# Padding one constant and the packs so that the large tiles begin at multiples of 128 bytes

## The chip, the core and the metric

The kernel runs on one core of one Trainium2 chip. The metric is the device time of one execution in microseconds, lower is better. The core has five engines with queues of their own: TensorE (PE in the profile; PEld is its loading of weights), VectorE (DVE), ScalarE (ACT), GpSimd (POOL) and SyncE (SP), which issues nearly all DMAs here.

## What is computed

A linear attention with a decay for each channel, over 4 sequences of 768 steps with 8 heads of 48 channels, and then two feed-forward layers on its 3072 rows of 384 numbers:

```python
for t in range(S):
    state = alpha[:, :, t, :, None] * state + np.einsum('bhd,bhe->bhde', k[:, :, t], v[:, :, t])
    y[:, :, t] = np.einsum('bhd,bhde->bhe', q[:, :, t], state)

h = x @ w_in                                   # layer 1: 384 -> 2048
x = np.maximum(0.01 * h, h) @ w_out            # 2048 -> 384
h = x @ w_in2                                  # layer 2, the same sizes
out = np.where(h > 0.0, h, np.exp(np.minimum(h, 0.0)) - 1.0) @ w_out2
```

The weights come as 64-bit floats, all else as 32-bit floats.

## The kernel before

**Feed-forward layers.** The 3072 rows are six blocks of 512 columns; the 2048 hidden channels are 16 slices of 128. Every number that goes into a product is split into a high and a low part, so each product takes three matmuls: high by high, low by high, high by low. One step (layer, block, slice) is nine matmuls into a bank `hp` (`ffn1_h`, L446; `ffn2_h`, L571), the nonlinearity and its split into `gh` and `gl` on ScalarE and VectorE, and nine matmuls from these into three banks (`ffn1_y`, L532; `ffn2_y`, L620; L635 in the very last block, with 384 columns). That is 864 matmuls for each product of each layer, 3456 in all, of which all but the last block's 144 have 512 columns (3312). Weights, `x`, `gh` and `gl` have the type fp32r (`F32R`), the attention's tiles plain 32-bit floats.

**Weights.** A slice of raw weights (3072 bytes per partition for each of its two matrices) is loaded into a staging tile (`stage1`, L720 to L722, five DMAs), turned into 32-bit floats by ScalarE and VectorE (p1, p2, and, j1, j2: L392, L397, L405, L408, L412) and split into the high and the low tile `w0_m`, `w1_m` (L415, L418). In layer 1, after the first four, slices take turns in the two staging tiles `x2t2` and `x2t3`; the second next slice can be loaded when L412 has read the present one.

**Attention.** A unit is 128 steps of one sequence, all heads; there are 24. Its decays, keys and queries come as one pack with 1541 floats per partition (`load_unit`, L121 on), its values as `vt` (`load_v`). The units 0 to 7 (`u < EARLY`) feed the first two blocks. From unit 8 on the pack is loaded in four DMAs, since two of the four head pairs have the halves of their keys swapped: L135 loads decays and the first keys, the two L138 the swapped halves, L139 the queries. Per unit, VectorE runs two scans (L169, L196) and scales keys and queries (L182 to L202), TensorE makes scores (`sc`, L211 and L274) and outputs, and ScalarE and VectorE write the result into an `x` tile. When a block's four units are done, `gather` (L385) moves rows of the `x` tile from partition to partition by DMA, six at once, and the block's L446 matmuls can begin. For the first two blocks SP issues every other one of the six, and ScalarE the rest. L360 subtracts the high part of the first blocks' outputs in the bank: one matmul whose 512 columns are four runs of 128 in an `x` tile.

**Order.** Up to about 340 us the order is written out by hand: the string `STARTUP` (L472) lists the steps, and every engine does its own ones in that order. Around the change SP's order is: the five loads of a slice, the pack and v of a unit (`more`), the next slice, the gather of a block. Each DMA is given one of eight completion semaphores in turn, so SP also waits, before a DMA, until the DMA eight earlier has landed.

**Tiles in memory.** A pool's tiles lie one behind the other in each partition, and each starts at the next multiple of 32 bytes. First come the constants (`ident`, `keep`, `d0`, `d1`, ..., `carried`, L62 to L70), then the 32 weight tiles, the six `x2t`, two `x` tiles, three `t`, two `gh`, two `gl`, three packs (also used for `span`, `stg` and `osb`), three `vt`, and the small ones of the attention (`pe`, `E`, `F`, `A`, `kn`, `S`, `T`). `carried` has 16 floats more than are written by L257, because L301 reads 64 columns from a head's 48. In the built program, bytes past a multiple of 128: weights, `x2t`, `x`, `t`, `gh`, `gl` 64; the three packs 64, 96 and 0; `vt` 32; `E` 0; `F` 32; `A`, `S` and `T` 64.

Of the kernel before, what the change touches and what calls it, by code (L numbers as in the profile page):

```python
# [8 lines left out]
F32 = mybir.dt.float32  # L9
# [10 lines left out]
def attention_two_layers_kernel(  # L20
# [12 lines left out]
    nc = tc.nc  # L33
    NT, DM = out.shape
    DFF = w1.shape[0] * 128
    D = HEAD_DIM
    H = DM // D
    C = CHUNK
    NU = NT // C
    NC = SEQ // C  # L40
    NP = H // 2
    PD = 2 * D
    PR = 64 + D
    KD = DM // 128
    KF = DFF // 128
    EXT = NP * (C + 1) + 1

    const = ctx.enter_context(tc.tile_pool(name="const", bufs=1))
    wts = ctx.enter_context(tc.tile_pool(name="wts", bufs=1))
# [4 lines left out]
    pack_p = ctx.enter_context(tc.tile_pool(name="pack", bufs=3))  # L54
# [8 lines left out]
    keep = const.tile([128, 2, C], I32, name="keep")  # L63
    d0 = const.tile([PR, EXT], F32, name="d0")
    d1 = const.tile([PR, EXT], F32, name="d1")
    bias = const.tile([PR, 2], F32, name="bias")
    outside = const.tile([PR, NU], F32, name="outside")
    far_sum = const.tile([PR, 2], F32, name="far_sum")
    near = const.tile([1, 1], I32, name="near")
    carried = const.tile([PR, NP * D + 16], F32, name="carried")  # L70

    both = [[wts.tile([128, 2 * DM], F32R, name=f"w{i}_{m}") for i in range(2)] for m in range(KF)]
    minus = both[KF - 1][0][0:PR, 0:PR]
# [22 lines left out]
    def constants():  # L96
# [4 lines left out]
        nc.vector.memset(d0, 0.0)  # L101
        nc.vector.memset(d0[:, 0:EXT:C + 1], 1.0)
        nc.vector.memset(d1, 0.0)
# [15 lines left out]
    st = {}  # L119

    def load_unit(u, first=False):  # L121
        t = pack_p.tile([PR, EXT + 2 * NP * C], F32, tag="pack", name="pack")
        if first:
            m = EXT + NP * C
            nc.sync.dma_start(t[:, 0:EXT], seqs[u, :, 0:EXT])
            nc.sync.dma_start(t[:, EXT:m], seqs[u, :, EXT:m])
            nc.sync.dma_start(t[:, m:], seqs[u, :, m:])
        elif u == 1:
            nc.sync.dma_start(t[:, 0:EXT], seqs[u, :, 0:EXT])
            nc.sync.dma_start(t[:, EXT:], seqs[u, :, EXT:])  # L130
        elif u < EARLY:
            nc.sync.dma_start(t, seqs[u])
        else:
            m, e = EXT + 2 * C, EXT + NP * C
            nc.sync.dma_start(t[:, 0:m], seqs[u, :, 0:m])  # L135
            dst, src = [a.rearrange("r (g h c) -> r g h c", g=2, h=2) for a in (t[:, m:e], seqs[u, :, m:e])]
            for h in range(2):
                nc.sync.dma_start(dst[:, :, h], src[:, :, 1 - h])  # L138
            nc.sync.dma_start(t[:, e:], seqs[u, :, e:])  # L139
        packs[u] = t  # L140

    def load_spare(u):
# [19 lines left out]

    def prep_E(u):
        t = packs.pop(u)
        al, kq = t if isinstance(t, tuple) else (t[:, 0:EXT], t[:, EXT:])
        kS = kq[:, 0:NP * C].rearrange("p (g c) -> p g c", c=C)
        qh = kq[:, NP * C:].rearrange("p (g c) -> p g c", c=C)
        E = at_p.tile([PR, EXT], F32, tag="E", name="E")
        nc.vector.tensor_tensor_scan(E[:, ::-1], al[:, ::-1], d0[:, ::-1], 0.0, ALU.mult, ALU.add)  # L169
        st[u] = dict(kS=kS, qh=qh, alpha=al, E=E)  # L170
# [17 lines left out]
    def prep_k(u):  # L188
        prep_E(u)
        prep_pe(u)  # L190
        prep_kS(u)
# [512 lines left out]
    def next_load(u):  # L704
        if u < NU:
            load_unit(u)
            load_v(u)
        else:
            t = pack_p.tile([128, 2 * 768], I32, tag="pack", name="stg")
            slots2.extend([(t[:, 0:768], 99), (t[:, 768:1536], 99)])  # L710
            fill2()
# [203 lines left out]

    with ExitStack():
        load_unit(0, True)
        constants()
        load_unit(1)
        load_v(0)  # L920
        load_unit(2)
# [26 lines left out]
        def early_h(j, m, ahead=0):  # L948
# [3 lines left out]

        first = {
            "E": prep_E, "pe": prep_pe, "kS": prep_kS, "F": prep_F, "q": prep_q, "sc": lambda u: (attn_scT if u >= EARLY else attn_sc)(u), "pk": attn_pk, "X": attn_X,
            "kn": attn_kn, "pu": attn_pu, "po": attn_po, "T": attn_T, "S": attn_state, "carry": attn_carry,
            "mask0": lambda u: mask_half(u, 0), "mask1": lambda u: mask_half(u, 1),
# [28 lines left out]
        for s, e in enumerate(seq):  # L985
            ph, j, m = e
# [13 lines left out]
            if after >= 0:  # L1000
                quota = 4 * 33 * (after + 1) // PACE - flow.n if after < PACE else 0
                if after == 0:
                    t = x2t[NT // 512 - 1].rearrange("p c f -> p (c f)").bitcast(I32)
# [38 lines left out]
            if ph == 2 and m >= KF - 10 and m % 2 == 0:  # L1042
                u = 5 * j + (m - KF + 10) // 2
# [95 lines left out]
```

## Time and profile before

| | us |
|---|---|
| median of 3 runs | 917.37 (916.95 to 919.85) |
| the profiled execution | 920.86 |
| its span, first to last instruction | 919.1 |
| TensorE busy | 892.4 |
| VectorE, ScalarE busy | 531.4, 455.6 |
| mean granted clock of TensorE | 0.995 of full speed |

TensorE is the engine with the most work, and the one whose instructions make up most of the chain that ended last. The first 150 us hold the attention's first units, the loads of the first layer's weights and their conversion, all at once; behind them TensorE works nearly without a break. "Busy" of TensorE is from start to a modelled end, and matmuls overlap; the spacing of two matmuls is read from their starts. A granted clock of 1.0 is 2.4 GHz, 0.5 is 1.2 GHz.

### The profile page before, as it was taken

The numbers are of one execution on the slowest core, as the hardware profiler recorded it, in microseconds if no ns is written. First come the engines' busy times: TensorE is split into PE (matmuls) and PEld (weight loads), VectorE is DVE, ScalarE is ACT, GpSimd is POOL, SyncE is SP. The second block draws the span as 40 slices with busy tenths as digits, with TensorE's granted clock in tenths as the row PEclk, the third lists the DMA queues.
The fourth block names the chain that finished last, engine by engine and source line by source line (L and its number), as shares of the span: only waits on it lengthen the run. The fifth ranks groups of instructions, "written<-read, shape, count | busy, mean of one in ns | idle before, by whom it ended". The sixth has DMA issues, their size and how long they took to land.

```text
span 919.1 us, 13668 instructions
## 1 busy us (share of the span) xinstructions
PE 892.4 (97%) x5306; PEld 735.0 (80%) x5306; DVE 531.4 (58%) x894; ACT 455.6 (50%) x841; POOL 11.8 (1%) x36
## 2 busy tenths in 40 slices
PE   8898999999899999989999999999999999999997
PEld 6676787888778877878888888888888888888896
DVE  8896888845564656455378888533443443443432
ACT  3476565332223222322367788656556565566442
POOL 1010000000000000000000000000000000000000
PEclk9999999999999999999999999999999999999999
DMA  9865452241113131221334241211200200300201
GB/s 223 201 173 153 129 147 78 65 101 44 44 44 79 44 87 28 52 78 36 103 90 117 74 116 48 41 37 29 55 11 21 54 11 21 55 20 1 36 1 38
DMA packets 69386, 64.01 MB, mean 70 GB/s; under 512 B 43904, under 2 KB 50560, under 8 KB 69312
## 3 DMA queue, kind: packets, MB, share of 16 engines
q1 hardware_dynamic: 68448, 61.87, 26.9%
q10 hardware_dynamic: 864, 1.18, 0.4%
q8 instruction: 44, 0.72, 0.3%
q14 instruction: 30, 0.25, 0.1%
HBM read 54.37 MB, written 4.72 MB: 64 GB/s over the span
## 4 chain that ended last, share of the span: by engine, by line
PE 82%; DVE 7%; DMA 6%; ACT 2%; SPq 1%; issue 1%; POOL 0%; DVEq 0%; ACTq 0%; POOLq 0%
PE hp L571 21%; PE y L532 17%; PE hp L446 16%; PE o L620 11%; PE oa L620 7%; PE oa L635 3%; DMA x2t<-in_w_dram 2%; PE po L292 2%; DMA vt<-in_vals_dram 2%; DMA pack<-in_seqs_dram 2%; PE sc L274 1%; DVE A L239 1%; DVE gl L464 1%; PE o L635 1%; ACT gh L460 1%
## 5 line engine op out<-in xcount | busy, mean ns | idle before, releaser
L446 PE MATMUL hp<-x,w 128*128 128x512 f32 x864 | 216.8, 393 | 4.0 <-DMA x<-x 2.6
L571 PE MATMUL hp<-x,w 128*128 128x512 f32 x864 | 212.3, 390 | 0.0
L446 PEld LDWEIGHTS hp<-x,w 128*128 128x128 f32 x864 | 161.9, 189 | 41.3 <-DMA x<-x 3.6
L571 PEld LDWEIGHTS hp<-x,w 128*128 128x128 f32 x864 | 161.9, 188 | 33.3 <-DVE w L418 0.2
L532 PE MATMUL y<-gh,w 128*128 128x512 f32 x576 | 170.2, 395 | 0.0
L584 DVE SCALAR_TENSOR_TENSOR t<-t,hp 128x512 f32<-128x512 f32 x96 | 65.9, 686 | 143.6 <-ACT t L579 143.1
L460 ACT CAST gh<-t 128x512 fp32r<-128x512 f32 x96 | 59.7, 623 | 144.9 <-PE y L532 103.7
L464 DVE TENSOR_TENSOR gl<-t,gh 128x512 fp32r<-128x512 f32 x96 | 65.9, 689 | 103.5 <-ACT gh L460 97.1
L532 PEld LDWEIGHTS y<-gh,w 128*128 128x128 f32 x576 | 106.1, 188 | 22.6 <-ACT gh L460 0.5
L595 DVE TENSOR_TENSOR gl<-t,gh 128x512 fp32r<-128x512 f32 x96 | 66.5, 693 | 66.5 <-ACT gh L589 66.5
L532 PE MATMUL y<-gl,w 128*128 128x512 f32 x288 | 102.6, 392 | 0.4 <-DVE gl L464 0.4
L451 ACT COPY t<-hp 128x512 f32<-128x512 f32 x96 | 56.2, 586 | 89.8 <-PE hp L446 84.3
L578 ACT ACTIVATE t<-hp 128x512 f32<-128x512 f32 x96 | 57.3, 597 | 80.9 <-PE hp L571 80.7
L589 ACT CAST gh<-t 128x512 fp32r<-128x512 f32 x96 | 59.7, 622 | 70.2 <-PE o L620 22.8
L620 PE MATMUL o<-gh,w 128*128 128x512 f32 x288 | 88.7, 389 | 0.1
L456 DVE SCALAR_TENSOR_TENSOR t<-t 128x512 f32<-128x512 f32 x96 | 65.5, 685 | 35.0 <-ACT t L451 34.8
L532 PEld LDWEIGHTS y<-gl,w 128*128 128x128 f32 x288 | 53.6, 188 | 12.7 <-DVE gl L464 1.4
L620 PEld LDWEIGHTS o<-gh,w 128*128 128x128 f32 x288 | 54.0, 188 | 11.6 <-ACT x2t L553 0.5
L579 ACT ACTIVATE t<-t 128x512 f32<-128x512 f32 x96 | 60.7, 632 | 3.1
L620 PE MATMUL oa<-gh,w 128*128 128x512 f32 x192 | 59.1, 389 | 0.0
L620 PE MATMUL o<-gl,w 128*128 128x512 f32 x144 | 56.0, 389 | 0.0
L620 PEld LDWEIGHTS oa<-gh,w 128*128 128x128 f32 x192 | 36.0, 188 | 7.4
(134 smaller groups left out, 883.8 us busy)
## 6 DMA issues: line engine op xcount, KB each, us to landing
stg<-in_w_dram SPq DMA_DIRECT2D x28, 384.0 KB, 3.1
x2t<-in_w_dram SPq DMA_DIRECT2D x20, 384.0 KB, 4.3
span<-in_seqs_dram SPq DMA_DIRECT2D x24, 226.2 KB, 2.6
pack<-in_seqs_dram SPq DMA_DIRECT2D x16, 338.2 KB, 3.4
x2t<-in_w_dram SPq DMA_DIRECT2D x32, 144.0 KB, 2.8
pack<-in_seqs_dram SPq DMA_DIRECT2D x18, 224.0 KB, 3.0
out_dram<-osb SPq DMA_DIRECT2D x60, 64.0 KB, 2.0
pack<-in_seqs_dram SPq DMA_DIRECT2D x5, 674.2 KB, 9.8
```

The source lines that it names most:

```text
L446: nc.tensor.matmul(hp, lhsT=a[:, kk, :], rhs=x[:, kk, :n], start=(0 in halves and i == 0), stop=(1 in halves and i == len(terms) - 1))
L456: nc.vector.scalar_tensor_tensor(out=t, in0=t, scalar=0.01, in1=t, op0=ALU.mult, op1=ALU.max)
L460: nc.scalar.copy(gh, steps["t", j, m])
L464: nc.vector.tensor_sub(gl, steps.pop(("t", j, m)), steps["gh", j, m].bitcast(F32))
L532: nc.tensor.matmul(ytiles[j][c], lhsT=a[:, c * 128:(c + 1) * 128], rhs=x, start=(first and 0 in halves and c not in begun), stop=(last and ...
L571: nc.tensor.matmul(hp, lhsT=a[:, kk, :], rhs=x[:, kk, :], start=(i == 0), stop=(i == 3 * KD - 1))
L578: nc.scalar.activation(t, hp, ACTF.Relu, scale=-1.0)
L579: nc.scalar.activation(t, t, ACTF.Exp, scale=-1.0)
L584: nc.vector.scalar_tensor_tensor(out=t, in0=t, scalar=-1.0, in1=hp, op0=ALU.add, op1=ALU.max)
L589: nc.scalar.copy(gh, t)
L595: nc.vector.tensor_sub(gl, t, gh.bitcast(F32))
L620: nc.tensor.matmul(otiles[j][c], lhsT=a[:, c * 128:(c + 1) * 128], rhs=x, start=(m == 0 and i == 0), stop=(m == KF - 1 and i == 2),)
```

## The change

`carried` gets 16 floats more, so that the tiles behind the constants begin 64 bytes later; and a pack's row gets 27 floats that nothing uses (1568 instead of 1541). The DMAs that wrote the whole tile now name its first 1541 floats. Nothing is computed otherwise.

```diff
+    END = EXT + 2 * NP * C
-    carried = const.tile([PR, NP * D + 16], F32, name="carried")
+    carried = const.tile([PR, NP * D + 32], F32, name="carried")
...
     def load_unit(u, first=False):
-        t = pack_p.tile([PR, EXT + 2 * NP * C], F32, tag="pack", name="pack")
+        t = pack_p.tile([PR, END + 27], F32, tag="pack", name="pack")
...
-            nc.sync.dma_start(t[:, m:], seqs[u, :, m:])
+            nc.sync.dma_start(t[:, m:END], seqs[u, :, m:])
...
-            nc.sync.dma_start(t[:, EXT:], seqs[u, :, EXT:])
+            nc.sync.dma_start(t[:, EXT:END], seqs[u, :, EXT:])
         elif u < EARLY:
-            nc.sync.dma_start(t, seqs[u])
+            nc.sync.dma_start(t[:, 0:END], seqs[u])
...
-            nc.sync.dma_start(t[:, e:], seqs[u, :, e:])
+            nc.sync.dma_start(t[:, e:END], seqs[u, :, e:])
...
-        al, kq = t if isinstance(t, tuple) else (t[:, 0:EXT], t[:, EXT:])
+        al, kq = t if isinstance(t, tuple) else (t[:, 0:EXT], t[:, EXT:END])
```

In the built program weights, `x2t`, `x`, `t`, `gh`, `gl`, packs and `vt` then begin at multiples of 128 bytes. The tiles behind them move too: `E` goes from 0 to 96 past such a multiple, `F` from 32 to 0, `A`, `S` and `T` from 64 to 32.

The order of the instructions stays the same on every engine, and so does what they do, but for a memset of `carried` with 32 instead of 16 columns. Waits change, because the builder finds other overlaps between two DMAs into one pack. On SP, at the load of unit 8 (here `pack_834`), before the change; `DMAHW0` to `DMAHW7` are the eight completion semaphores, and each DMA's own is the first one named where it waits for the DMA eight earlier:

```order
L135 DMA pack_834<-in_seqs_dram 112x773 [waits DMAHW3_49,PE_49]
L138 DMA pack_834<-in_seqs_dram 112x2x64 [waits DMAHW4_49]
L138 DMA pack_834<-in_seqs_dram 112x2x64 [waits DMAHW5_49,DMAHW4_49]
L139 DMA pack_834<-in_seqs_dram 112x512 [waits DMAHW6_49]
L155 DMA vt_839<-in_vals_dram 128x2x144 [waits DMAHW7_49]
L157 DMA vt_839<-in_vals_dram 64x288 [waits DMAHW0_49]
L157 DMA vt_839<-in_vals_dram 64x288 [waits DMAHW1_49]
L720 DMA x2t3_138<-in_w1_dram 48x768 [waits DMAHW2_49,DVE_49]
```

And with the change (lines are one further on):

```order
L136 DMA pack_834<-in_seqs_dram 112x773 [waits DMAHW3_49,PE_49]
L139 DMA pack_834<-in_seqs_dram 112x2x64 [waits DMAHW4_49]
L139 DMA pack_834<-in_seqs_dram 112x2x64 [waits DMAHW5_49]
L140 DMA pack_834<-in_seqs_dram 112x512 [waits DMAHW6_49]
L156 DMA vt_839<-in_vals_dram 128x2x144 [waits DMAHW7_49]
L158 DMA vt_839<-in_vals_dram 64x288 [waits DMAHW0_49]
L158 DMA vt_839<-in_vals_dram 64x288 [waits DMAHW1_49]
L721 DMA x2t3_138<-in_w1_dram 48x768 [waits DMAHW2_49,DVE_49]
```

The second of the two half-swapped loads waited for `DMAHW4`, on which the first one lands; now it does not. It is so for each of the units 8 to 23. On TensorE, the scores of unit 9 (`pack_1029`), before:

```order
L274 MATMUL sc0_1301<-pack_1029 64x128
L274 MATMUL sc1_1302<-pack_1029 64x128
L274 MATMUL sc0_1301<-pack_1029 64x128 [waits DMAHW1_49,DMAHW0_49]
L274 MATMUL sc1_1302<-pack_1029 64x128
L274 MATMUL sc0_1301<-pack_1029 64x64
L274 MATMUL sc1_1302<-pack_1029 64x64
```

and with the change:

```order
L275 MATMUL sc0_1301<-pack_1029 64x128
L275 MATMUL sc1_1302<-pack_1029 64x128
L275 MATMUL sc0_1301<-pack_1029 64x128 [waits DMAHW1_49]
L275 MATMUL sc1_1302<-pack_1029 64x128
L275 MATMUL sc0_1301<-pack_1029 64x64 [waits DMAHW0_49]
L275 MATMUL sc1_1302<-pack_1029 64x64
```

The wait for one of the two loads stands two matmuls later, at the first that reads what it brings.

## Rows read from the trace of the kernel before

**Rows 1.** The page: busy time of each engine; shares of the chain that ended last.

```profile
PE 892.4 (97%) x5306; PEld 735.0 (80%) x5306; DVE 531.4 (58%) x894; ACT 455.6 (50%) x841; POOL 11.8 (1%) x36
...
PE 82%; DVE 7%; DMA 6%; ACT 2%; SPq 1%; issue 1%; POOL 0%; DVEq 0%; ACTq 0%; POOLq 0%
```

**Rows 2.** Stretches from:to, their length, busy us of each engine, clock, DMA.

```profile
core 0: us, PE busy (x) PEld busy (x) DVE busy (x) ACT busy (x) POOL busy (x), PEclk, DMA share, GB/s
...
70.60:77.40 6.80, 4.25 (x11) 2.82 (x11) 2.19 (x4) 2.72 (x4) 0.00 (x0) 0.75 0.71 170
77.40:97.00 19.60, 19.60 (x88) 16.17 (x88) 15.71 (x22) 12.25 (x20) 0.48 (x1) 1.00 0.59 163
97.00:125.00 28.00, 26.60 (x140) 20.29 (x139) 24.40 (x35) 19.94 (x32) 0.00 (x0) 1.00 0.36 106
125.00:146.00 21.00, 20.74 (x91) 16.65 (x90) 17.43 (x26) 12.35 (x19) 0.32 (x1) 1.00 0.50 140
```

**Rows 3.** The chain that ended last, 20 to 78 us: start, us, what.

```profile
21.17 9.46 DMA pack<-in_seqs_dram
...
30.65 10.09 DMA vt<-in_vals_dram
...
57.54 4.57 DMA pack<-in_seqs_dram
...
63.47 4.87 DMA vt<-in_vals_dram
...
68.83 4.44 DMA x<-x
...
73.32 4.08 PE hp L446 x9
```

**Rows 4.** Two stretches of TensorE alone: length, busy (matmuls), clock, DMA.

```profile
73.60:76.90 3.30, 3.30 (x8) 0.50 0.70 194
560.00:640.00 80.00, 80.00 (x353) 1.00 0.18 40
```

**Rows 5.** Waits of SP's queue: us in total, times, longest.

```profile
SPq L138 <- DMA pack<-in_seqs_dram: 48.2, 16, 4.7
```

**Rows 6.** SP's queue in time: start, us, what.

```profile
57.54 4.92 SPq L138 DMA_DIRECT2D pack<-in_seqs_dram  x2
...
64.78 0.52 SPq L720 DMA_DIRECT2D x2t<-in_w_dram  x1
...
67.69 0.42 SPq L722 DMA_DIRECT2D x2t<-in_w_dram  x1
```

**Rows 7.** ScalarE in time: start, us, what, [idle before, ended by].

```profile
65.55 0.59 ACT L364 CAST x<-po 112x512 fp32r<-112x512 f32 x1 [0.58 <-PE po L360]
...
66.55 0.91 ACT L397 ACTIVATE x2t<-x2t 128x768 int32<-128x768 uint16 x1
67.90 2.50 ACTq L385 DMA_DIRECT2D x<-x  x3
72.67 0.89 ACT L392 ACTIVATE x2t<-x2t 128x768 f32<-128x768 f32 x1 [5.21 <-DMA x<-x]
```

**Rows 8.** VectorE in time, around the same place.

```profile
61.26 0.96 DVE L412 CUSTOM_DVE_ANT_0 x2t<-x2t,x2t 128x1536 uint16<-128x1536 uint16 x1
...
74.07 0.69 DVE L456 SCALAR_TENSOR_TENSOR t<-t 128x512 f32<-128x512 f32 x1 [3.75 <-ACT t L451]
```

**Rows 9.** TensorE in time: one L360 and the matmul that follows.

```profile
55.65 0.40 PE L360 MATMUL po<-x,w 112*112 112x512 f32 x1
55.89 0.26 PE L219 MATMUL pk<-ident,pack 112*128 112x112 f32 x1
```

**Rows 10.** One line's instructions, L196, 200 to 345 us: ns min/median/max, first and last start.

```profile
L196 DVE TENSOR_TENSOR_SCAN F<-pack,d x7: 1222/1224/1227, 222.7 to 337.8; 112x516 f32<-112x516 f32 x7
```

**Rows 11.** The same view of L813, loads into the packs' slots, 595 to 830 us.

```profile
L813 SPq DMA_DIRECT2D span<-in_seqs_dram x19: 312/313/447, 599.6 to 823.2; - x19
...
DMA to landing us min/median/max: 2.4/2.6/2.8
```

**Rows 12.** The page's groups: matmuls of both layers, busy and mean ns, idle before.

```profile
L446 PE MATMUL hp<-x,w 128*128 128x512 f32 x864 | 216.8, 393 | 4.0 <-DMA x<-x 2.6
L571 PE MATMUL hp<-x,w 128*128 128x512 f32 x864 | 212.3, 390 | 0.0
```

## The prediction

> **What bounds the kernel now.** The first view is the page's busy times and the shares of its chain [rows 1]: TensorE works 892.4 of 919.1 us and holds 82% of the chain that ended last. So only two things can move the end: what each matmul takes, and the 26.7 us in which TensorE idles. The second view, the stretches [rows 2], says where it idles early on: in 70.60 to 77.40 TensorE is busy 4.25 of 6.80 us and its mean granted clock is 0.75; in 77.4 to 97 it is busy all of the time; it idles 1.40 us in 97 to 125, and 0.26 in 125 to 146. The third, the chain [rows 3], names who held it in the first of these: a pack load issued at 57.54, a v load at 63.47, the gather x<-x at 68.83 and then nine matmuls at 73.32 that take 4.08 us. Eight matmuls in 73.6 to 76.9 ran at a granted clock of 0.50, which is the 1.2 GHz level, after TensorE had idled 2.55 us [rows 2, 4]. The fourth view is one long steady stretch [rows 4]: 353 matmuls in 80.00 us, 226.6 ns each, where 512 columns at one a cycle and 2.4 GHz are 213.3 ns: 13.3 ns too many, and the place where a start of 64 bytes past a multiple of 128 could hide.
>
> **Part 1, the waits that go.** The padded pack row changes what the builder takes for overlapping. For each of the 16 units from 8 on, the second of the two half-swapped key loads (L138) no longer waits until the first has landed. SP held 48.2 us in that wait, 16 times [rows 5]. What it is worth depends on who waits behind it.
>
> The first one, at 57.54. SP is in the two L138 issues for 4.92 us, all but some 0.8 of it the wait; behind it stand the rest of the pack, v, weight slice 5 (L720 to L722) and SP's half of the gather [rows 6]. Without the wait SP comes to L720 at about 60.3. There it waits for DVE's L412 to free the staging tile, 61.26 + 0.96 = 62.2 [rows 8], so slice 5 starts at 62.25 instead of 64.78, and its last load (67.69 before) goes out near 64.1 [rows 6]. The gather's source is written by ACT's L364, done at 65.55 + 0.59 = 66.1; SP can issue its half from there instead of 68.83 [rows 3, 7]. ACT issues the other half and is free only at 66.55 + 0.91 = 67.5, against 67.90 [rows 7]. So ACT's half now comes last. How long it takes to land: 4.44 us before, behind slice 5's big load [rows 3]; 2.6, the median of a load in a quiet stretch [rows 11], at best. Slice 5 would be 3.5 us ahead, so I take 2.9, nearer the quiet row: landing near 70.4 (between 70.1 and 71.9). TensorE's work ahead of it is done at 73.32 - 2.55 = 70.8. Of the 2.55 us of idle time, between 1.3 and all goes; I take 2.4. With no idle stretch ahead of it the clock should stay at the higher level, which gives back 4.08 - 2.04 (nine times 226.6 ns) = 2.04 us, or nothing if it falls anyway. Together 4.4 (1.3 to 4.6).
>
> Who is late next? ACT waited 5.21 us for slice 5 before L392 at 72.67, and DVE 3.75 behind it [rows 7, 8]; both start about 3.4 us earlier now. TensorE gains 4.4, so it may have to wait up to 1.0 for them; two banks for hp give it 2.04 us of work in between. I take off 0.7: **3.7 us (1.0 to 4.6)**.
>
> The second and third waits, at 83 and 125, stand while TensorE is full (19.60 of 19.60, 20.74 of 21.00 [rows 2]): worth nothing by themselves. But weight slices arrive earlier behind them, which feeds ACT and DVE in 97 to 146, where TensorE idles 1.66 us in all. Between 0 and 1.7; I take 0.5. The other 13 stand after 146, where units are loaded well ahead: 0. The wait that moves two matmuls later on TensorE meets a DMA long landed: 0.
>
> **Part 2, the starts of the tiles, on TensorE.** Weights, x, gh and gl go from 64 bytes past a multiple of 128 to 0. Is that the 13.3 ns? If a read went in pieces of 128 bytes, 2048 bytes from 64 would take 17 pieces where 16 would do, and one piece is 32 columns, 13.3 ns: the number fits exactly. But one kind of matmul tests it: L360 reads its 512 columns as four runs of 512 bytes, each starting at 64, and would take 20 pieces, 267 ns. The next matmul starts 0.24 us after it (55.65 and 55.89 [rows 9]). So the 13.3 ns comes once per matmul and not once per start; I take 0 for the change, and keep the rest as a rival.
>
> The Trainium skill ("TensorE: Matmul & The Clock Gate", Back-to-back issue gap) gives N / 2.4 + 2.5 ns for a warm gap, 215.8 ns for 512 columns, and measured it on bf16. This trace has 226.6, so the measurement decides here; by that rule, if the starts were the whole difference, the change would be worth 36 us on 3312 matmuls and end near 877.
>
> **Part 3, the starts on the other engines and DMA.** Packs already lie at three different starts (64, 96 and 0 past 128; 192, 224 and 0 past 256), and units take them in turn. Seven scans over the three take 1222 to 1227 ns, and 19 loads into them land in 2.4 to 2.8 us [rows 10, 11]. So the starts cost VectorE nothing, and by its nearness I take nothing for ScalarE. For DMA the spread is 0.2 around 2.6, 8% either way: on the pack and v loads of 9.46 and 10.09 us that stand in the chain before 42 us [rows 3] that is up to 1.5 us better or worse; I take 0.
>
> The Trainium skill ("DMA: Bandwidth & Descriptors", How a descriptor splits into AXI transactions) lets a transaction start only at multiples of 256 bytes, so a 3072-byte row from 192 would be 13 of them instead of 12. By that rule the early loads would be some 8% shorter, which is the better end of the bound just given; the loads into three starts show no such order.
>
> Sum: 3.7 + 0.5 = 4.2 us off, between 1.0 - 1.5 = -0.5 and 4.6 + 1.7 + 1.5 = 7.8. The profiled execution took 920.86 (span 919.1) and would take 916.7; it lay 0.4% above the median of the runs, 917.37. Taken off the median: **913.2**.
>
> **Rivals.** *The head start is given back* (no change, 917.4, or 915 to 919): TensorE comes 4 us earlier to slices whose weights DVE and ACT have not split yet, and idles there instead. For it: DVE is busy 24.40 of 28.00 us in 97 to 125, ACT 19.94 [rows 2]. Against it: both sat idle 3.75 and 5.21 us for the same late loads. Unprofiled runs that never dropped the clock at 73.6 would also have only half of it to gain.
>
> *TensorE's 13.3 ns was the start after all* (869): 3312 x 13.3 ns = 44 us, and the 4.2. For it stands the fit of 32 columns; against it L360.
>
> *TensorE's reads collide* (slower, 923): all big tiles, packs and v now begin at the same place modulo 128, where packs and v lay at 96, 0 and 32 before. The matmuls of the first layer, among pack and v traffic, already last 393 ns where the second layer's last 390 [rows 12]. Another 3 ns on 3312 matmuls costs 9.9 us, against the 4.2. It decides for slower from (4.2 + 2.75) / 3312 = 2.1 ns per matmul. Against it: weights, x and g keep their distances from each other, as they all move by 64.
>
> *The change does not do what it says*: the built program has the starts at 0 as stated, so this is out.
>
> **How the numbers follow.** 0.3%, about what a measurement of this kernel can tell from no change, is 2.75 us. Forecast (4.2 off, 2.8 to 7.8): 0.55. Given back, or only half of it real: 0.27. The 13.3 ns gone: 0.08. Collisions or DMA made worse: 0.10. Faster 0.55 + 0.08 = 0.63, same 0.27, slower 0.10. The range leaves out the 869 and most of the slower case, and reaches from the sum's better end, 917.4 - 7.8 = 909.6, over no change to 919.4, where the given-back case (2 us worse at most) ends.
>
> **What would show it.** Right: in the changed kernel SP issues both L139 loads back to back near 57.5; TensorE starts the matmuls after the gather near 70.7 with no idle stretch, nine of them in 2.04 us, and no stretch at clock 0.50 near 74; ACT's L393 no longer idles 5 us before it; in steady stretches 226.6 ns per matmul stays, and the scans stay at 1225. Wrong: a pitch below 220 (the starts were it) or above 228 (collisions); or the same start at 70.7 but idle time that comes back between 77 and 146.

## The result, and the profile after

The changed kernel took 909.49 us (median of 4 runs, 908.50 to 911.75) against 918.23 us for the kernel before (4 runs, 916.95 to 919.85): a ratio of 0.9914, 95% interval 0.9887 to 0.9940, or 8.7 us off. In a second comparison it took 911.42 us (12 runs, 909.94 to 915.79) against 917.40 (23 runs, 914.50 to 920.83): 0.9942, 0.9923 to 0.9961, 6.0 us off. So it is faster, as both intervals leave out no change. The first interval, 5.5 to 10.4 us off, lies above the 4.2 us of the forecast; the second, 3.6 to 7.1, holds them.

The first comparison's profiled execution of the change took 911.75 us, its span is 910.0. The page of the changed kernel (its line numbers are one higher than before's), as [rows 1] of before:

```profile
PE 887.2 (97%) x5306; PEld 733.5 (81%) x5306; DVE 531.6 (58%) x894; ACT 455.8 (50%) x841; POOL 11.8 (1%) x36
...
PE 87%; DVE 5%; DMA 4%; SPq 1%; ACT 1%; issue 1%; POOL 0%; DVEq 0%; ACTq 0%; POOLq 0%
```

TensorE's busy time fell by 5.2 us, and its share of the chain rose from 82 to 87%. The stretches of the changed kernel, as [rows 2, 4] (from:to, length, busy us of each engine, clock, DMA):

```profile
57.50:70.60 13.10, 13.10 (x96) 10.57 (x97) 12.41 (x20) 8.88 (x16) 2.62 (x1) 1.00 0.72 195
70.60:77.40 6.80, 6.80 (x32) 5.63 (x31) 5.32 (x8) 5.25 (x8) 0.00 (x0) 1.00 0.60 158
77.40:97.00 19.60, 19.60 (x89) 16.21 (x88) 17.93 (x28) 14.41 (x22) 0.48 (x1) 1.00 0.58 148
97.00:125.00 28.00, 27.44 (x147) 22.01 (x146) 24.59 (x34) 18.09 (x28) 0.32 (x1) 1.00 0.61 165
125.00:146.00 21.00, 21.00 (x161) 17.48 (x160) 18.15 (x28) 11.83 (x18) 0.00 (x0) 1.00 0.19 60
560.00:640.00 80.00, 80.00 (x354) 66.06 (x353) 35.56 (x56) 50.46 (x91) 0.00 (x0) 1.00 0.15 34
```

The stretch 70.6 to 77.4 is full, at a granted clock of 1.00, with 32 matmuls begun where [rows 2] had 11 at 0.75. The steady stretch has not moved: 354 matmuls in 80.00 us, as the 353 of [rows 4]. So nothing happened to a matmul itself.

How the wait's end travels through the queues is seen on four engines. SP in time, changed kernel:

```profile
56.03 0.93 SPq L139 DMA_DIRECT2D pack<-in_seqs_dram  x2
57.00 0.45 SPq L140 DMA_DIRECT2D pack<-in_seqs_dram  x1
...
60.71 0.33 SPq L721 DMA_DIRECT2D x2t<-in_w_dram  x1
...
62.48 1.76 SPq L723 DMA_DIRECT2D x2t<-in_w_dram  x1
64.63 2.38 SPq L386 DMA_DIRECT2D x<-x  x3
```

VectorE in time:

```profile
59.72 0.96 DVE L413 CUSTOM_DVE_ANT_0 x2t<-x2t,x2t 128x1536 uint16<-128x1536 uint16 x1
...
69.18 0.69 DVE L457 SCALAR_TENSOR_TENSOR t<-t 128x512 f32<-128x512 f32 x1 [0.39 <-ACT t L452]
```

ScalarE in time:

```profile
64.02 0.59 ACT L365 CAST x<-po 112x512 fp32r<-112x512 f32 x1 [0.58 <-PE po L361]
...
64.64 0.61 ACTq L386 DMA_DIRECT2D x<-x  x1
65.02 0.91 ACT L398 ACTIVATE x2t<-x2t 128x768 int32<-128x768 uint16 x1
65.29 1.25 ACTq L386 DMA_DIRECT2D x<-x  x2
67.75 0.92 ACT L393 ACTIVATE x2t<-x2t 128x768 f32<-128x768 f32 x1 [1.82 <-DMA x2t<-in_w_dram]
```

The six DMAs of that gather (L386, 60 to 76 us), where before has 4.3/4.7/5.0:

```profile
DMA to landing us min/median/max: 3.0/3.4/3.9
```

TensorE in time, at the gather and where [rows 2] idled in 97 to 125:

```profile
68.28 0.94 PE L533 MATMUL y<-gl,w 128*128 128x512 f32 x3
69.06 4.27 PE L447 MATMUL hp<-x,w 128*128 128x512 f32 x18
...
92.89 1.52 PE L447 MATMUL hp<-x,w 128*128 128x512 f32 x6
```

The two swapped loads go out in 0.93 us, where [rows 6] has 4.92. Weight slice 5 starts at 60.71, right when L413 has freed the staging tile (59.72 + 0.96), and SP's half of the gather at 64.63, right when L365 has written its source (64.02 + 0.59): the two limits that the prediction had named as next. The matmuls after the gather follow the ones before without idle time, eighteen of them in one piece, where [rows 3] has the gather in the chain and nine in 4.08 us.

**A ruler for the rest.** The 5306 matmuls come in the same order in all the kernels here, so the start of the n-th one (counted from 0) can be compared between traces. Number 400 starts near 45 us, 614 is the last one ahead of the gather's matmuls and 622 the eighth of these, and 713 to 940 covers 97 to 146 us in before. Times between starts, in us:

| profile | start of 400 | 400 to 614 | 614 to 622 | 622 to 713 | 713 to 800 | 800 to 940 | 940 to last | 400 to last |
|---|---|---|---|---|---|---|---|---|
| before | 46.65 | 23.72 | 6.18 | 20.89 | 22.45 | 26.46 | 766.16 | 865.84 |
| before, again | 44.32 | 23.72 | 6.19 | 21.48 | 22.19 | 26.99 | 766.07 | 866.65 |
| the change | 45.14 | 23.69 | 1.85 | 20.63 | 20.63 | 25.79 | 766.02 | 858.60 |
| the change, again | 44.24 | 23.70 | 1.85 | 20.63 | 21.21 | 25.79 | 766.12 | 859.30 |
| waits only | 49.96 | 23.72 | 1.83 | 20.63 | 20.55 | 25.76 | 766.21 | 858.71 |
| waits only, again | 43.58 | 24.17 | 1.94 | 20.65 | 21.05 | 25.76 | 766.07 | 859.64 |
| starts at 96, no waits | 43.54 | 23.70 | 1.84 | 20.63 | 20.95 | 25.75 | 766.29 | 859.16 |
| first wait gone | 43.61 | 23.86 | 1.83 | 20.63 | 21.95 | 25.90 | 766.14 | 860.31 |
| first wait kept | 43.52 | 23.72 | 6.04 | 21.62 | 20.93 | 25.76 | 766.14 | 864.21 |
| starts only, all waits | 47.27 | 23.71 | 5.30 | 20.90 | 22.07 | 25.80 | 766.18 | 863.95 |

The last column parts the kernels cleanly: 866.2 on average for before, 858.6 to 859.6 for every kernel without the waits, whatever its starts. The difference of the means is 7.2 us: 4.3 at the gather, 0.6 up to matmul 713, 1.4 and 1.0 in the two columns after it, less 0.1 ahead of the gather, and nothing behind matmul 940. The column that scatters is the first: at matmul 400 the two profiles of before differ by 2.3 us, those of the change by 0.9, and those of the waits-only kernel by 6.4.

### The profile page after: what moved, and what is told of

Read it like the earlier page. It is cut to its first block, busy times and chain, and to the rows that moved or that the text cites. A ratio compares the mean times of both kernels' runs of the same rounds, so it can differ in the third digit from the quotient of the medians.

```text
span 910.0 us, 13650 instructions
## 1 busy us (share of the span) xinstructions
PE 887.2 (97%) x5306; PEld 733.5 (81%) x5306; DVE 531.6 (58%) x894; ACT 455.8 (50%) x841; POOL 11.8 (1%) x36
## 4 chain that ended last, share of the span: by engine, by line
PE 87%; DVE 5%; DMA 4%; SPq 1%; ACT 1%; issue 1%; POOL 0%; DVEq 0%; ACTq 0%; POOLq 0%
PE hp L572 21%; PE y L533 19%; PE hp L447 18%; PE o L621 11%; PE oa L621 7%; DMA pack<-in_seqs_dram 3%; PE oa L636 3%; PE po L293 2%; PE sc L275 1%; DVE A L240 1%; PE o L636 1%; PE pk L220 1%; PE po L302 1%; DMA x2t<-in_w_dram 1%; DVE gl L465 1%
## 5 line engine op out<-in xcount | busy, mean ns | idle before, releaser
L457 DVE SCALAR_TENSOR_TENSOR t<-t 128x512 f32<-128x512 f32 x96 | 65.6, 686 | 31.7 <-ACT t L452 31.5
```

The source lines that it names most:

```text
L457: nc.vector.scalar_tensor_tensor(out=t, in0=t, scalar=0.01, in1=t, op0=ALU.mult, op1=ALU.max)
```

## The experiments

**Waits without starts.** The constant keeps its size, and the packs get one float instead of 27: all tiles begin where they did before, and the sixteen waits are gone as in the change. The diff against the changed kernel:

```diff
-    carried = const.tile([PR, NP * D + 32], F32, name="carried")
+    carried = const.tile([PR, NP * D + 16], F32, name="carried")
-        t = pack_p.tile([PR, END + 27], F32, tag="pack", name="pack")
+        t = pack_p.tile([PR, END + 1], F32, tag="pack", name="pack")
```

> The pack row gets one float more instead of 27 and the constant none, so every tile begins where it did before (64 bytes past a multiple of 128 for weights, x, gh and gl), and the 16 waits for the first of two half-swapped loads are gone as in the change. If the waits are the whole gain: 909.5 us, 8.7 below before, and a trace like that of the change. If the starts bring the part that came before 57 us (1.3 us, the clock that does not fall at 36 us): 910.8. If the starts are most of it: 916 or more.

Measured: 911.99 us (7 runs), ratio to before 0.9951 (0.9927 to 0.9976), beside 25 runs of before at 917.41. Its profiled execution was a long one, 917.06. The stretch from 18.0 to 34.8 us in it says why (columns as above):

```profile
18.00:34.80 16.80, 16.62 (x135) 13.41 (x136) 10.03 (x17) 4.86 (x11) 0.80 (x2) 0.50 0.83 198
```

TensorE had 1.2 GHz for 17 us of its startup, and matmul 400 began 3.3 us later than in before. From there to the end it took 858.71 us, the 858.60 of the change. By its time alone the 2.5 us between it and the change's 909.49, from another comparison, could be the starts; the runs beside the change further on decide that.

**Starts without waits.** The constant is enlarged as in the change, and the packs of the units before 8 are padded, while the others use the whole row. All tiles begin where they do in the change, and all sixteen waits are there. Against the changed kernel:

```diff
-        t = pack_p.tile([PR, END + 27], F32, tag="pack", name="pack")
+        t = pack_p.tile([PR, END + (27 if u < EARLY else 0)], F32, tag="pack", name="pack")
```

> All tiles begin at the multiples of 128 as in the change, but packs of units 8 to 23 keep their row of 1541 floats in the larger slot, so all waits stay as before. If the waits are the whole gain: 918.2, within 0.3% of before. If the starts bring the 1.3 us before 57 us: 916.9. If they are most of it: 911 or less. If the starts cost TensorE anything, matmuls are spaced by more than 226.6 ns in 560 to 640 us.

Measured: 916.37 us (12 runs), ratio 0.9987 (0.9969 to 1.0005): no change that can be told. SP's waits in it, and its stretches (columns as above):

```profile
SPq L139 <- DMA pack<-in_seqs_dram: 43.1, 16, 3.8
```

```profile
57.50:77.40 19.90, 18.05 (x121) 14.01 (x120) 15.09 (x23) 11.91 (x22) 2.62 (x1) 0.91 0.65 178
...
560.00:640.00 80.00, 80.00 (x354) 65.99 (x353) 38.55 (x63) 52.18 (x95) 0.00 (x0) 1.00 0.17 40
```

With every big tile at a multiple of 128 the matmul still takes 226 ns, and idle time and a lowered clock stand at the gather as before. The ruler's 863.95 is 2.3 below before; 0.9 of it lies at the gather and 1.2 between matmuls 713 and 940, where before's two profiles differ by 0.3 and 0.5 from each other in the two columns. That a small part of this is the starts' is not excluded by the interval, which reaches to 2.8 us; no other kernel shows it. The column 800 to 940 has 25.80 here, as without the waits, though all of them are kept; that counts further down.

**The first wait alone.** Two kernels with all starts as before part the sixteen waits. In one only unit 8's pack is padded, so that only its wait goes; in the other all but unit 8's are:

```diff
-    carried = const.tile([PR, NP * D + 32], F32, name="carried")
+    carried = const.tile([PR, NP * D + 16], F32, name="carried")
-        t = pack_p.tile([PR, END + 27], F32, tag="pack", name="pack")
+        t = pack_p.tile([PR, END + (u == EARLY)], F32, tag="pack", name="pack")
```

> Tiles begin where they did before; of the 16 waits only the first, at unit 8 (58 us), is gone. If that one brings what the prediction took from it, some 4 us of idle time and clock, and the others nothing: 914. If the two later ones at 83 and 125 us bring the 2.5 us that the change gained between 77 and 125: 912 here and the rest with the others. If the head start is lost without them: 917.

The other has `END + (u != EARLY)` in the same place.

> Tiles begin where they did before; the first wait, at unit 8, stays, and the other 15 are gone. If only the first one counts: 918.2. If those at 83 and 125 us feed VectorE and ScalarE earlier and so spare TensorE the 1.7 us that it idles in 97 to 146 us: 916.5. If the two parts simply add to the 8.7 us: this and the run with the first one gone come to 8.7 us together.

Measured: first wait gone 912.17 us (7 runs), ratio 0.9952 (0.9934 to 0.9970); first wait kept, fifteen gone, 913.52 (12 runs), 0.9970 (0.9949 to 0.9991). SP's waits in the two, 15 and 1 of 16:

```profile
SPq L139 <- DMA pack<-in_seqs_dram: 43.4, 15, 4.3
```

```profile
SPq L139 <- DMA pack<-in_seqs_dram: 3.5, 1, 3.5
```

The stretches with the first wait gone:

```profile
57.50:77.40 19.90, 19.90 (x127) 16.46 (x127) 17.64 (x26) 14.33 (x23) 2.62 (x1) 1.00 0.71 182
77.40:97.00 19.60, 18.52 (x81) 14.63 (x80) 16.01 (x25) 12.58 (x20) 0.48 (x1) 1.00 0.46 122
97.00:125.00 28.00, 27.96 (x150) 22.31 (x149) 25.21 (x35) 18.50 (x29) 0.32 (x1) 1.00 0.51 148
```

And with it kept:

```profile
57.50:77.40 19.90, 16.84 (x104) 13.18 (x102) 13.21 (x21) 10.36 (x16) 2.62 (x1) 0.91 0.56 130
77.40:97.00 19.60, 19.60 (x88) 16.21 (x88) 17.24 (x25) 14.91 (x25) 0.48 (x1) 1.00 0.63 172
97.00:125.00 28.00, 27.14 (x146) 21.78 (x145) 24.52 (x35) 17.55 (x27) 0.00 (x0) 1.00 0.50 139
```

One SP wait of some 4 us decides whether 57.5 to 77.4 is full at 1.00 or has 3 us of idle time and a clock of 0.91. By the ruler the first wait alone is worth 866.2 - 860.3 = 5.9 us, the others 866.2 - 864.2 = 2.0; together 7.9, against 7.2 with all gone. By the medians, with startup and scatter in them, it is 5.2 and 3.9 (interval 0.8 to 4.7). The two parts overlap a little between matmuls 713 and 940: with the first wait gone these take 1.2 us less than before, with the others gone 2.4, and with all gone 2.4. This is one profile each, and before's two differ there by some tenths.

**The change again, beside three others.** Four kernels ran on one chip: the change, waits only, one with other starts and no waits, and before. The third has weights, staging tiles, `x`, `t`, `gh` and `gl` at 96 bytes past a multiple of 128:

```diff
-    carried = const.tile([PR, NP * D + 32], F32, name="carried")
+    carried = const.tile([PR, NP * D + 24], F32, name="carried")
-        t = pack_p.tile([PR, END + 27], F32, tag="pack", name="pack")
+        t = pack_p.tile([PR, END + 19], F32, tag="pack", name="pack")
```

> The changed kernel once more, beside three others on one chip. Theory (only the waits act, the starts act on nothing): a time within 0.2% (1.8 us) of the kernel with the waits gone and the old starts, about 910 to 912, and a ratio to the kernel before of 0.990 to 0.996; after the first 45 us TensorE gains 7 to 8 us on the kernel before. Rival (the new starts are worth 2 us or more, since the first comparison gave 909.5 for the change and 912.0 for the waits alone): 2 us or more below the kernel with the waits alone also on this chip.

> Waits gone, all starts as before, once more beside the changed kernel. Theory: 910 to 912.5, within 1.8 us of the changed kernel; 353 or 354 matmuls in 560 to 640 us; if no stretch at clock 0.50 falls into its first 45 us its span is that of the changed kernel within 1 us (the first profile had 17 us at 0.50 there, and lost some 7 us by it). Rival (starts matter): 2 us or more above the changed kernel, with the loss growing along the span.

> Waits gone, and weights, staging tiles, x, t, gh and gl at 96 bytes past a multiple of 128 (where the change has 0 and the kernel before 64). Theory: 226.6 ns per matmul in 560 to 640 us as in all others, and the time of the changed kernel within 1.8 us, 910 to 912. Rival (a start at 0 is better than any other): at least 2 us above the changed kernel, near the kernel with the waits alone or worse; a read that went in pieces of 128 bytes would show as a pitch that is not 226.6.

> The kernel before, profiled and timed once more. Theory: 916 to 918.5; TensorE idles 2 to 3 us before the matmuls that follow the gather near 73 us and then has a stretch at granted clock 0.50 of about 3.4 us there, as in both profiles that keep the first wait; stretches at 0.50 in the first 45 us differ from profile to profile in length and place. Rival (that stretch near 73 us was an accident of one profile, and only the idle time is lost): no stretch at 0.50 between 70 and 80 us, and the matmuls after the gather at 227 ns each.

| kernel | median us (runs) | ratio to the 23 runs of before, 917.40 | interval |
|---|---|---|---|
| the change | 911.42 (12) | 0.9942 | 0.9923 to 0.9961 |
| waits only | 910.17 (6) | 0.9931 | 0.9915 to 0.9947 |
| starts at 96, no waits | 910.44 (6) | 0.9937 | 0.9919 to 0.9954 |
| before | 918.22 (12) | 1.0009 | 0.9995 to 1.0024 |

The three kernels without the waits lie within 1.25 us, and the change is the slowest of them: the starts are worth nothing that these runs can tell. The steady stretch with starts at 96, and then with waits only, where they are at 64:

```profile
560.00:640.00 80.00, 80.00 (x354) 65.97 (x353) 35.23 (x55) 49.63 (x90) 0.00 (x0) 1.00 0.15 33
```

```profile
560.00:640.00 80.00, 80.00 (x353) 65.99 (x352) 35.30 (x56) 50.15 (x90) 0.00 (x0) 1.00 0.16 34
```

Starts of 0, 64 and 96 give one pitch. The rule of the Trainium skill that the prediction weighed ("TensorE: Matmul & The Clock Gate", Back-to-back issue gap) would be 215.8 ns; no profile here comes near it, so for these fp32r matmuls the measurement stands.

Before, profiled again, TensorE at the gather in time, and then the stretch in which its clock was low:

```profile
70.95 0.73 PE L446 MATMUL hp<-x,w 128*128 128x512 f32 x2 [2.52 <-DMA x<-x]
72.21 6.88 PE L446 MATMUL hp<-x,w 128*128 128x512 f32 x22 [0.53 <-DMA x<-x]
```

```profile
73.00:74.90 1.90, 1.90 (x6) 1.51 (x5) 0.75 (x1) 0.61 (x1) 0.00 (x0) 0.50 0.69 207
```

Idle time of 3.05 us and then a clock of 0.50 again. All four profiles of kernels that keep the first wait (before twice, starts only, first wait kept) have a stretch of 3.4 us at 0.50 there, and none of the six others has one.

## Why the prediction was right, and what it mis-sized

**The first wait: the route held but for one step, and the size came out as 4.9 to 5.9 instead of 3.7 us.** The prediction had slice 5 starting at 62.25 and the gather's source ready at 66.1; the changed profile, which was 1.5 us ahead at matmul 400 already, has 60.71 and 64.61, so both to 0.1 us. TensorE's gain at the gather was put at 4.4 (2.4 of idle time, 2.04 of clock), and the ruler's column 614 to 622 has 4.3.

That the two agree so well is in part luck. The prediction let ScalarE's half of the gather go last, at 67.5, when ScalarE is done with L397. In the changed profile ScalarE's queue issues that half from 64.64 on, when the source has just been written, while L398 only starts at 65.02; SP's half is the one that goes last. What held ScalarE's half until 67.90 in before was not L397, done at 67.46: the queue waits at L385 until 67.85 for a completion semaphore, and the v load issued at 63.00 lands on it at 67.83. SP's half starts behind the next v load in the same way [rows 3], and both of these loads had come late by the first wait. The landings then took 3.0 to 3.9 us where the prediction took 2.9, so the last of the six DMAs landed at 69.47, or 71.0 by before's time, not at 70.4. TensorE lost nothing by it, as its first matmuls behind the gather wait for the first pair of the six alone: that had landed at 68.57, and TensorE came to it at 68.83. In the second profile of the change it is 66.84 and 67.94.

The step that failed is the 0.7 taken off because ScalarE and VectorE would be late next. They did start as much earlier as forecast: L393 at 67.75 against 72.67 and L457 at 69.18 against 74.07 [rows 7, 8], 4.9 us, of which 1.5 are the startup and 3.4 the wait. But TensorE did not wait for them at all; the eighteen matmuls at 69.06 run on. Instead of a loss there was a further gain, for which the prediction had no term: 0.6 us up to matmul 713, nearly all of it the rest of the stretch at 1.2 GHz (matmuls 0.43 us apart behind number 622, where the change has 0.23). With the first wait alone gone there are 1.2 us more behind 713 (22.32 + 26.73 - 21.95 - 25.90). Of these 0.8 lie behind matmul 800, where the kernel with all waits and new starts is as fast, so they can't be put down to this wait with certainty. The 4.3 and the 0.6 alone exceed the bound of 4.6.

**The second and third waits: 2.0 us instead of 0.5, over the bound of 1.7.** The route was the one named, weight slices that arrive late, and it is shown for the second wait: the four profiles that keep it have 21.95 to 22.45 us in the column 713 to 800, the six others 20.55 to 21.21. Of the 2.0 us 1.4 lie there. The second wait is seen in SP's queue of the kernel before:

```profile
82.51 4.97 SPq L138 DMA_DIRECT2D pack<-in_seqs_dram  x2
...
92.25 0.37 SPq L720 DMA_DIRECT2D x2t<-in_w_dram  x1
...
94.06 0.42 SPq L722 DMA_DIRECT2D x2t<-in_w_dram  x1
```

ScalarE in time, kernel before:

```profile
96.17 0.92 ACT L397 ACTIVATE x2t<-x2t 128x768 int32<-128x768 uint16 x1 [4.47 <-DMA x2t<-in_w_dram]
...
99.42 0.60 ACT L451 COPY t<-hp 128x512 f32<-128x512 f32 x1
```

And TensorE:

```profile
100.08 1.65 PE L446 MATMUL hp<-x,w 128*128 128x512 f32 x6 [0.78 <-ACT t L451]
...
102.10 0.97 PE L532 MATMUL y<-gl,w 128*128 128x512 f32 x3 [0.37 <-DVE gl L464]
```

SP is in the two L138 issues for 4.97 us at 82.51, two weight slices stand behind them, of which the second is issued from 92.25 to 94.48, ScalarE idles 4.47 us for it and then has the copy `t` of a bank behind a backlog, and TensorE waits for that copy at 100.08. In the changed kernel the same matmuls (92.89) show no idle time. The split of the waits shows that this stall is not the first wait's: with the first kept and the others gone the matmul starts 0.23 us after the one before it, with only the first gone 1.12 us after it, and in before 1.17. Of the other fifteen, the one at 82.51 is the one ahead of it. ScalarE with only the first wait gone still idles for the slice:

```profile
88.54 0.92 ACT L398 ACTIVATE x2t<-x2t 128x768 int32<-128x768 uint16 x1 [4.34 <-DMA x2t<-in_w_dram]
```

With the first kept and the others gone it never idles for a slice between 86 and 102 us. The waits that moved on TensorE are no rival here: L274, where they stand, first runs at 122.9 us.

For the third wait the runs decide less. The 1.0 us of the column 800 to 940 are short waits for ScalarE in before: for weights that it has just split (L415) at 145.76, and in its second profile at 144.33, and there also for `gh` (L460) at 141.00. But with the new starts and all waits kept the column has 25.80 us, and with only the first wait gone 25.90, where before has 26.46 and 26.99. So these waits are all but gone also where the third wait stays, and no run shows that it costs anything by itself.

The bound was made from the idle column of [rows 2], 1.40 + 0.26. That column counts idle time from the modelled end of a matmul; by the starts, the matmul at 100.08 comes 0.94 us late where the column says 0.78, and small delays behind it (0.33 and 0.34 us where 0.23 is the pitch) show in no column. The starts of the matmuls would have given the whole: in before 713 to 940 takes 48.91 us and with no waits 46.3 to 47.0. A part of the gain is given back a little later: the matmul at 113.15 in before starts 0.61 us after the one ahead of it, and the same one 0.95 us in the change and 1.50 in its second profile.

**The other waits: nothing, as forecast.** From matmul 940 to the last one all ten profiles have 766.0 to 766.3 us.

**The starts: nothing that these runs can tell, as forecast.** On TensorE the pitch is the same for starts of 0, 64 and 96, so the 13.3 ns above 213.3 are not the starts'. That they come once per matmul, as the prediction argued from L360, is borne out by the last block: its matmuls of 384 columns mostly start 173 ns apart, and at the rate of 512 in 213.3 ns they would be 160 apart, so 13 ns are over there too. What they are is open. On the other engines, the scan of [rows 10] in the changed kernel (L197, 200 to 345 us):

```profile
L197 DVE TENSOR_TENSOR_SCAN F<-pack,d x7: 1226/1227/1229, 214.1 to 329.2; 112x516 f32<-112x516 f32 x7
```

And the loads of [rows 11] (L814):

```profile
DMA to landing us min/median/max: 2.4/2.6/2.8
```

Nothing has moved. But the loads of [rows 11] could not test the 256-byte rule that the prediction took from the Trainium skill ("DMA: Bandwidth & Descriptors", How a descriptor splits into AXI transactions). By an estimate from that rule a row of L813, 2068 bytes, is nine transactions from each of the three starts, and a whole pack row of 6164 bytes is 25; so no order was to be expected, and the early pack loads would not have become 8% shorter. The weight slices' rows of 3072 bytes would, with 12 transactions for 13. Their 20 loads of 384 KB, number and median landing in us, in before and then with starts only:

```profile
x2t<-in_w_dram SPq DMA_DIRECT2D x20, 384.0 KB, 4.3
```

```profile
x2t<-in_w_dram SPq DMA_DIRECT2D x20, 384.0 KB, 4.2
```

The change has 4.0 and 4.1 in its two profiles, and waits only, with the old starts, 4.0 and 4.2. These differ among themselves by as much as 8%, so a gain is neither shown nor excluded for a single load; in the time of the starts-only kernel there is none that can be told.

**The rivals.** That the head start is given back is out: 7.2 us are still there at the end. A remark in it, that executions whose clock does not fall gain less, stays open. The ten profiles have a mean granted clock of 0.997 or less if the clock fell at the gather or in the startup, and 0.998 or 0.999 if it did not. Of the 35 runs of before in the second comparison, the four at 0.999 have a median of 915.0; of the change's 12, the six at 0.999 have 910.4. That is 4.6 us, and 7.2 less the half of a 3.4 us stretch would be 5.5. But of the 25 runs of before beside the first four experiments, the six at 0.999 have 916.2, little below the 917.4 of all. Without a trace the mean clock does not say where it fell, and no profile of before shows an execution in which it stayed up at the gather. The other two rivals, a pitch below 220 or above 228 ns, did not occur.

**The sum.** 4.2 us were forecast; 7.2 are there by the ruler, and 8.7 and 6.0 by the medians of the two comparisons. The first median, 909.49, lies 0.1 us below the better end of the prediction's range, 909.6, and the second inside it. The direction and the source of the gain were right, and the starts were rightly put at nothing; the size was too small because the waits' consequences behind the gather were taken as a loss or as next to nothing. The intervals of the two comparisons overlap. A part of their difference may be the clock of the first 45 us: of the 12 runs of the change in the second one, the three with a mean clock of 0.993 to 0.995 took 914.7 to 915.8 us, while the four runs of the first were all at 0.998 or 0.999. Where in these runs the clock fell isn't shown.

## What to carry to other kernels

SP's queue issues everything in order here, and a wait in it was as dear as the most urgent transfer behind it: sixteen waits summed to 48 us, the first of them cost 5 to 6, the second some 1.4, and the thirteen behind 146 us nothing. When a layout change is to be judged, compare the waits that the built program has before and after as well as the addresses; here one unused float in a tile's row did what 27 did. And size such a term from the starts of a fixed sequence of instructions rather than from an idle column, and look for late arrivals a few steps further on before taking anything off.

## What the runs showed that was not expected

- **The clock near the start.** The time at 1.2 GHz in the first 45 us differs between executions of nearly the same program: none in seven of the ten profiles, 3.4 us in two (36.0 to 39.4 in before, 42.6 to 46.1 in starts only), 17.1 us in one (17.8 to 34.9 in waits only). Matmul 400 starts between 43.5 and 50.0 us, latest in the profile with 17.1 us; this is nearly as much as the whole change is worth. What sets it off was not settled.
- **After idle time the clock fell in every case seen at one place**: 1.9 to 3.1 us without a matmul at the gather, in one piece or in two, and 3.4 us at 0.50, in four profiles of four that keep the first wait; half of 3.4 us is the price on top of the idle time. The pauses of 1.3 us later on, six between 220 and 412 us in every profile, were followed by no such stretch.
